# Attention scores as plain float32 products on 64-row halves of the TensorE array

## The chip, the cores and the metric

The kernel runs on one core of one Trainium2 chip. The metric is the device time of one execution in microseconds. A core has five engines that matter here: TensorE (PE; its weight loads are listed apart as PEld), VectorE (DVE), ScalarE (ACT), GpSimd (POOL) and SyncE (SP), whose queue issues most of the DMA transfers.

## The reference

Block-causal attention over 8 batches of 8 heads, 576 positions and 64 features, and behind it a feed-forward network on the 4608 tokens of 512 features, with 2048 hidden features and a leaky activation with a slope per hidden feature.

```python
scores = scale * np.matmul(q, k.transpose(0, 1, 3, 2))     # scale = 1/8
mask = block_i >= block_j                                  # blocks of 64 positions
scores = np.where(mask, scores, -1000000000.0)
scores = scores - np.max(scores, axis=-1, keepdims=True)
attn = np.exp(scores)
attn = attn / (np.sum(attn, axis=-1, keepdims=True) + 1e-09)
out = np.matmul(attn, v)
...
h = x @ w_in
g = np.maximum(h, 0.0) + alpha * np.minimum(h, 0.0)
return (g @ w_out).astype(np.float32)
```

Everything is float32. q and k are scaled so that the scores are large enough for their rounding to be seen in the output.

## The kernel before

**Tiling.** The 64 heads are taken as 32 pairs (p = 0 to 31, four pairs to a batch). A pair lies on the 128 partitions: features of head 0 on 0 to 63, of head 1 on 64 to 127. Queries are taken in tiles of 128 (j = 0 to 3), and a tile j sees the first w = 128 (j + 1) keys. The last 64 queries of both heads form one more tile, j = 4, which sees all 576 keys: q comes from the host with these 64 columns of head 0 zero on the rows of head 1 and the reverse, so that one product with all 128 rows gives both heads.

**One query tile** (`query_tile`): scores into PSUM banks, row maximum on VectorE (L897 or L903), exponential on ScalarE (L906), row sums and reciprocal on VectorE, scaling by it on GpSimd (L914), transposes on TensorE (L922), copies to PTF. Then `values` multiplies the transposed probabilities with v (L1022): both heads of a pair, each on its own 64 columns of the array, as plain float32 products, and the result goes to xT, from where the feed-forward network takes it.

**Scores of most pairs.** A float32 product can be made of several products of the faster type float32r, if each operand is split into a rounded part and a remainder. `prep` loads q and k of a pair, writes QH (q/8 rounded, ScalarE, L781), QL (the remainder, VectorE, L783), KH (ScalarE, L786) and KL (GpSimd, L787), and then moves these by ten DMA transfers on SP's queue (`move`, L791) into two stacked tiles Q and K. There each head has all 128 rows of the array: one product (L890, i = 0) adds QH KH and QL KH, a second (i = 1) adds QH KL and, from its other 64 rows, the mask (`late` and `here`, written once into Q and K by `fixed_parts`). So a score tile j below 4 takes two float32r products per head. The tile j = 4 takes six of 288 columns straight from QH, QL, KH and KL (L952).

**Scores of the first pairs.** So that the start need not wait for all this, the tiles j = 0 and 1 of pairs 0 to 3, and all tiles of pair 0, are made as plain float32 products (`plain`): q is loaded into parts of xT that are free then, each head in its own 256 columns with zeros on the other head's rows (`early_loads`, `rest`), k is scaled by 1/8 (`scaled`: on VectorE for pairs 0 and 1, L805, on GpSimd for the others, L807), the product uses all 128 rows of the array (L885), and the mask is added by a small bfloat16 product (L886). The last tile of pair 0 is at L946.

**Banks.** There are eight PSUM banks; at most 7 of them may be held by attention, 2 by hidden activations, 2 by output sums. For j < 2 the two heads' scores share a bank, for j = 2 and 3 each has its own.

**The order.** All work is entered as operations with an engine, an estimated cost, a priority, what they read and write, and the buffers that they claim. A planner (`Plan.schedule`) simulates the engines with these costs and issues on each engine the ready operation with the lowest priority number. A table, SHIFTS, adds an offset to the priority of single operations; its keys are the priorities before the offset. The costs of products on part of the array are estimated by `c_apart(n, more)`. The part of the feed-forward network with the hidden slices f = 0 to 5 of 16 (FA = 6, in chunks of 256 tokens, `ffn1` L623 and `ffn2` L660) is issued between the attention products while later pairs are still being worked on; the rest (L701, L660) runs after attention, from about 575 us.

Weights arrive as 64-bit numbers and are converted by `to_f32` (the DMA at L505, then VectorE and ScalarE), two blocks at a time.

Of the kernel before, what the change touches and what calls it, by code (L numbers as in the profile page):

```python
# [373 lines left out]
def attn_ffn(ctx, tc, qT, kT, vT, w_in, w_out, alpha, out):  # L374
# [20 lines left out]
    nc.vector.memset(mask_l[0:1, 0:64], 1.0)  # L395
    nc.vector.memset(mask_r[0:1, :], NEG)
# [21 lines left out]
    KX = pool0.tile([P, 384], F32, name="KX")  # L418
# [3 lines left out]
    sp = att.enter_context(tc.tile_pool(name="sp", bufs=1))  # L422
# [20 lines left out]
    def rooms(pool, *kinds):  # L443
        for kind, n, shape, dt in kinds:
# [4 lines left out]
    rooms(st, ("qraw", 1, [QP], F32), ("kraw", 1, [S], F32), ("vraw", 1, [5, 2, D], F32), ("p", PB, [512], F32), ("pl", 1, [S], F32),  # L449
# [3 lines left out]
    late = const.tile([P, 8], F32, name="late")  # L453
    here = const.tile([P, 8], F32, name="here")
    nc.gpsimd.memset(late, 0.0)
    nc.gpsimd.affine_select(out=late, in_=late, pattern=[[1, 8]], base=64, channel_multiplier=-1,
                            compare_op=ALU.is_ge, fill=NEG)
    nc.gpsimd.memset(here, 0.0)
    nc.gpsimd.affine_select(out=here, in_=here, pattern=[[1, 8]], base=64, channel_multiplier=-1,
                            compare_op=ALU.not_equal, fill=1.0)  # L460

    def spread(t):

        ap = t[64:128]
        return bass.AP(ap.tensor, ap.offset, [ap.ap[0], [0, 2], [1, 8], [0, 64]])
# [302 lines left out]
    def twice(ap):  # L768
        return bass.AP(ap.tensor, ap.offset, [ap.ap[0], [0, 2], [1, SM]])

    def prep(p, pr):


        raw, kraw, vraw = Buf("qraw"), Buf("kraw"), Buf("vraw0" if p % 2 else "vraw")
        QH, QL, KH, KL, Q, K = (Buf(k) for k in ("QH", "QL", "KH", "KL", "Q", "K"))
        op("SP", 320, lambda: nc.sync.dma_start(out=raw(), in_=qT[p]), w=[raw], prio=pr)
        op("SP", 288, lambda: nc.sync.dma_start(out=kraw(), in_=kT[p]), w=[kraw], prio=pr)
        op("SP", 320, lambda: nc.sync.dma_start(out=vraw(), in_=vT[p]), w=[(vraw, 0), (vraw, 1)], prio=pr + VL)
        v_parts = vraw, [(vraw, 0), (vraw, 1)]

        op("ACT", c_act(QP, True), lambda: nc.scalar.activation(out=QH(), in_=raw(), func=AF.Copy, scale=0.125),  # L781
           r=[raw], w=[QH], prio=pr)
        op("DVE", c_dve(QP), lambda: nc.vector.scalar_tensor_tensor(  # L783
            out=QL(), in0=raw(), scalar=0.125, in1=QH().bitcast(F32), op0=ALU.mult, op1=ALU.subtract),
            r=[raw, QH], w=[QL], prio=pr)
        op("ACT", c_act(S, True), lambda: nc.scalar.copy(out=KH(), in_=kraw()), r=[kraw], w=[KH], prio=pr)  # L786
        op("POOL", c_pool(S), lambda: nc.gpsimd.tensor_tensor(  # L787
            out=KL(), in0=kraw(), in1=KH().bitcast(F32), op=ALU.subtract), r=[kraw, KH], w=[KL], prio=pr)

        def move(to, of, key, src, kb=128):  # L790
            op("SP", kb, lambda: nc.sync.dma_start(out=to().bitcast(F32), in_=of().bitcast(F32)), r=[src], w=[key], prio=pr)  # L791
        for h in range(2):
            hs, qs = slice(64 * h, 64 * h + 64), slice(SM * h, SM * h + SM)
            move(lambda qs=qs: Q()[0:64, :, qs], lambda hs=hs: twice(QH()[hs, :SM]), (Q, h, 0), QH, 256)
            move(lambda qs=qs: Q()[64:128, 0, qs], lambda hs=hs: QL()[hs, :SM], (Q, h, 1), QL)
            for i in range(2):
                ro = slice(64 * i, 64 * i + 64)
                move(lambda h=h, ro=ro: K()[ro, 2 * h], lambda hs=hs: KH()[hs, :SM], (K, h, i), KH)
            move(lambda h=h: K()[0:64, 2 * h + 1], lambda hs=hs: KL()[hs, :SM], (K, h, 2), KL)
        qk_parts = (Q, K, (QH, QL, KH, KL))  # L800
        return qk_parts, v_parts

# [6 lines left out]

    def early_loads():  # L810


        def zeros(engine, ps):
            for h in range(2):
                rows = slice(64 - 64 * h, 128 - 64 * h)
                engine.memset(xT[rows, ps, S + 256 * h:S + 256 * h + 256], 0.0)
        pr = E0 - 8
        op("DVE", 700, lambda: zeros(nc.vector, slice(0, 1)), w=[("zeros", 0)], prio=pr)
        op("POOL", 1600, lambda: zeros(nc.gpsimd, slice(1, NP)), w=[("zeros", p) for p in range(1, NP)], prio=pr)

        def tails():
            for h in range(2):
                nc.gpsimd.memset(KX[64 - 64 * h:128 - 64 * h, 256 + 64 * h:320 + 64 * h], 0.0)
        op("POOL", 400, tails, w=[("zeros", "tail")], prio=pr + 1)
        for p0, p1 in ((0, 1), (1, NP)):
            for h in range(2):
                hs = slice(64 * h, 64 * h + 64)
                op("SP", 64 * (p1 - p0), lambda h=h, hs=hs, p0=p0, p1=p1: nc.sync.dma_start(
                    out=xT[hs, p0:p1, S + 256 * h:S + 256 * h + 256],
                    in_=qT[p0:p1, hs, :256].rearrange("p r n -> r p n")), w=[("q", p, h) for p in range(p0, p1)], prio=pr)  # L830
        for ps, to, queue in (((0,), lambda: o_k()[:, :256], "ACTQ"), ((1, 2), lambda: o_k2().rearrange("p (i n) -> p i n", i=2), "SP"),
                              ((3,), lambda: KX[:, :256], "SP")):
            issuer = {"SP": nc.sync, "ACTQ": nc.scalar}[queue]
            op(queue, 128 * len(ps), lambda ps=ps, to=to, issuer=issuer: issuer.dma_start(
                out=to(), in_=kT[ps[0]:ps[-1] + 1, :, :256].rearrange("p r n -> r p n") if len(ps) > 1 else kT[ps[0], :, :256]),
                w=[("k", p) for p in ps], claim=[o_k] if ps == (0,) else [o_k2] if len(ps) > 1 else [], prio=pr + ps[0])
        for p in range(NP):
            scaled(p, 256, lambda p=p: plain_k[p]()[:, :256], ("k", p), pr + p)

    def early(p, pr):  # L840
        vraw = Buf("vraw0" if p % 2 else "vraw")
        op("SP", 128, lambda: nc.sync.dma_start(out=vraw()[:, :2], in_=vT[p, :, :2]), w=[(vraw, 0), (vraw, 1)], prio=pr + VE)
        return None, (vraw, [(vraw, 0), (vraw, 1)])

    def rest(pr):

        vraw = Buf("vraw")
        for h in range(2):
            hs = slice(64 * h, 64 * h + 64)
            op("SP", 64, lambda h=h, hs=hs: nc.sync.dma_start(out=xT[hs, 0, S + 256 * h:S + 256 * h + 256], in_=qT[0, hs, 256:512]),  # L850
               w=[("q", 0, h)], prio=pr)
        op("SP", 128, lambda: nc.sync.dma_start(out=o_k()[:, 256:512], in_=kT[0, :, 256:512]), w=[("k", 0, 1)], claim=[o_k], prio=pr)
        scaled(0, 256, lambda: o_k()[:, 256:512], ("k", 0, 1), pr)
        op("SP", 32, lambda: nc.sync.dma_start(out=klast(), in_=kT[0, :, 512:S]), w=[("k", 0, 2)], prio=pr)
        scaled(0, 64, klast, ("k", 0, 2), pr)
        for h in range(2):
            hs = slice(64 * h, 64 * h + 64)
            op("SP", 16, lambda h=h, hs=hs: nc.sync.dma_start(out=KX[hs, 256 + 64 * h:320 + 64 * h], in_=qT[0, hs, SM + 64 * h:SM + 64 * h + 64]),
               w=[("tail", h)], prio=pr)
        op("SP", 320, lambda: nc.sync.dma_start(out=vraw(), in_=vT[0]), w=[(vraw, 0), (vraw, 1)], prio=pr + VL)  # L860
        return None, (vraw, [(vraw, 0), (vraw, 1)])

    def query_tile(p, qk_parts, j, pr):
# [307 lines left out]
```

## Time and profile before

| | us |
|---|---|
| time, median of 3 runs | 1109.04 |
| lowest and highest of the runs | 1108.87, 1112.01 |
| span of the profiled execution | 1112.3 |
| attention stage with network work between | 0 to about 575 |
| rest of the network | about 575 to 1112 |

The profiled execution's own time is given by its span alone, 1112.3 us; it is near the highest of the three timed runs.

A page of the profile has the busy time of each engine, a strip of 40 slices of the span, the chain of work that ended last, and the costliest groups of instructions, named by line, engine, operation and tiles. A group `bank<-K,Q 128*128 128x512 f32 x4` is four instructions on an array of 128 rows by 128 columns with 512 moving columns. A float32 product stands as two records, a float32r product as one; the trace writes f32 for both. Products are pipelined, and the ends of their records are modelled: the distance from one start to the next is what a product costs.

### The profile page before, as it was taken

How to read it: one execution, taken by the hardware profiler on the slowest of the kernel's cores; microseconds unless marked ns; L12 is line 12 of the kernel's file. 1: busy time of each engine (PE TensorE's matmuls, PEld its weight loads, DVE VectorE, ACT ScalarE, POOL GpSimd, SP SyncE). 2: the span in 40 equal slices, each digit the busy share in tenths (PEclk: the TensorE clock that was granted, in tenths of full speed). 3: DMA queues.
4: the chain of work that ended last, by engine and by line, in shares of the span. 5: the costliest groups of instructions: out<-in, count | busy, mean ns of one | idle time of the engine just before them, and what ended most of it. 6: DMA issues, size and time to landing. Idle time of an engine off the chain costs nothing.

```text
span 1112.3 us, 21554 instructions
## 1 busy us (share of the span) xinstructions
PE 1091.3 (98%) x7342; PEld 949.8 (85%) x7342; DVE 700.1 (63%) x1651; ACT 627.4 (56%) x1740; POOL 600.2 (54%) x771
## 2 busy tenths in 40 slices
PE   7989999999999999999999999999999999999998
PEld 5668888888888888888888888889898989898987
DVE  7787666565565655756548997564747555555554
ACT  7878877675676676757655655343433434343432
POOL 5657657655656555555569985343434435252522
PEclk9999999999999999999999999999999999999999
DMA  7897787766476774738343523130303030312021
GB/s 219 239 260 226 198 244 187 208 186 183 127 203 189 192 209 124 230 103 244 80 148 114 165 90 103 43 114 1 115 1 114 1 114 7 108 39 77 1 76 39
DMA packets 75309, 147.92 MB, mean 133 GB/s; under 512 B 9792, under 2 KB 11840, under 8 KB 75200
## 3 DMA queue, kind: packets, MB, share of 16 engines
q1 hardware_dynamic: 74768, 146.28, 44.9%
q8 instruction: 58, 0.95, 0.4%
q14 instruction: 51, 0.42, 0.1%
q10 hardware_dynamic: 432, 0.27, 0.1%
HBM read 68.40 MB, written 29.36 MB: 88 GB/s over the span
## 4 chain that ended last, share of the span: by engine, by line
PE 89%; DVE 3%; DMA 3%; POOL 2%; issue 1%; SPq 1%; ACT 0%; DVEq 0%; POOLq 0%
PE bank L660 34%; PE bank L701 20%; PE bank L623 12%; PE bank L1022 7%; PE bank L890 6%; PE bank L922 6%; DMA raw<-in_w_in 2%; PE bank L952 2%; PE bank L978 1%; DVE m L507 1%; DMA raw<-in_w_out 1%; POOL xl L611 0%; POOL w L529 0%; DVE m L519 0%; DVE bank L512 0%
## 5 line engine op out<-in xcount | busy, mean ns | idle before, releaser
L643 POOL TENSOR_TENSOR gl<-g,gh 128x256 fp32r<-128x256 f32 x288 | 220.9, 776 | 303.7 <-ACT gh L640 159.3
L701 PEld LDWEIGHTS bank<-X,w 128*128 128x128 f32 x1890 | 246.1, 189 | 16.6 <-DVE X L529 1.2
L701 PE MATMUL bank<-X,w 128*128 128x256 f32 x1890 | 250.7, 281 | 1.1 <-DVE X L529 1.0
L660 PE MATMUL bank<-w,gh 128*128 128x512 f32 x720 | 225.3, 394 | 0.0
L634 ACT ACTIVATE g<-bank 128x256 f32<-128x256 f32 x288 | 109.5, 384 | 197.2 <-DVE bank L714 164.0
L914 POOL TENSOR_SCALAR p<-p,ri 128x128 f32<-128x128 f32 (+3 forms) x256 | 137.6, 552 | 126.7 <-DVE ri L912 56.4
L636 DVE SCALAR_TENSOR_TENSOR g<-g,oal,bank 128x256 f32<-128x256 f32 x288 | 134.3, 476 | 57.9 <-ACT g L634 55.3
L640 ACT CAST gh<-g 128x256 fp32r<-128x256 f32 x288 | 116.4, 407 | 89.7 <-DVE g L636 85.5
L906 ACT ACTIVATE p<-bank,nm 128x256 f32<-128x256 f32 (+3 forms) x256 | 133.8, 530 | 34.9 <-DVE nm L903 15.5
L660 PE MATMUL bank<-w,gl 128*128 128x512 f32 x360 | 141.6, 393 | 0.0
L714 DVE TENSOR_TENSOR bank<-bank,g 128x256 f32<-128x256 f32 x180 | 75.0, 428 | 102.7 <-PE bank L701 99.0
L660 PE MATMUL bank<-wa,gh 128*128 128x512 f32 x432 | 139.6, 404 | 0.0
L660 PEld LDWEIGHTS bank<-w,gh 128*128 128x128 f32 x720 | 124.0, 188 | 17.4
L623 PE MATMUL bank<-xh,wa 128*128 128x256 f32 x864 | 128.1, 287 | 0.9 <-DVE PTF L996 0.7
L623 PEld LDWEIGHTS bank<-xh,wa 128*128 128x128 f32 x864 | 113.8, 190 | 4.5 <-DVE PTF L996 1.1
L922 PE MATMUL bank<-ident,p 128*128 128x128 f32 x640 | 100.6, 278 | 9.3 <-POOL p L914 7.4
L890 PE MATMUL bank<-K,Q 128*128 128x512 f32 (+1 forms) x472 | 100.1, 332 | 0.8 <-DMA K<-KL 0.7
L922 PEld LDWEIGHTS bank<-ident,p 128*128 128x128 f32 x640 | 76.0, 142 | 21.6 <-POOL p L914 12.1
L710 DVE TENSOR_TENSOR g<-bank,g 128x256 f32<-128x256 f32 x135 | 56.6, 421 | 59.6 <-PE bank L701 58.4
L1022 PE MATMUL bank<-PTF,vraw 128*64 128x320 f32 (+3 forms) x768 | 94.1, 384 | 0.0
L903 DVE TENSOR_REDUCE nm<-bank 128x1 f32<-128x512 f32 (+1 forms) x128 | 76.4, 617 | 23.0 <-PE bank L890 19.0
L660 PE MATMUL bank<-wa,gl 128*128 128x512 f32 x216 | 85.5, 396 | 0.5 <-POOL gl L643 0.4
(111 smaller groups left out, 1677.8 us busy)
## 6 DMA issues: line engine op xcount, KB each, us to landing
Q<-QH SPq DMA_DIRECT2D x62, 256.0 KB, 3.8
K<-KH SPq DMA_DIRECT2D x124, 128.0 KB, 3.7
vraw<-in_v SPq DMA_DIRECT2D x32, 320.0 KB, 4.2
qraw<-in_q SPq DMA_DIRECT2D x31, 320.0 KB, 3.8
xd<-xT SPq DMA_DIRECT2D x8, 1152.0 KB, 6.7
part<-o SPq DMA_DIRECT2D x36, 256.0 KB, 3.0
xb<-xd SPq DMA_DIRECT2D x9, 1024.0 KB, 5.4
m<-part SPq DMA_DIRECT2D x36, 256.0 KB, 2.9
```

What stands on the lines that cost most here:

```text
L623: nc.tensor.matmul(hp()[:, :n], ww()[:, 0, cc * P:(cc + 1) * P], x()[:, cc, :n], start=(i == 0 and cc == 0), stop=(i == 2 and cc == NCC - 1))
L634: op("ACT", c_act(CHA), lambda: nc.scalar.activation(out=g(), in_=hp()[:, ts], func=AF.Relu, scale=-1.0), r=[hp], w=[g], prio=FP)
L636: op("DVE", c_dve(CHA) + 60, lambda: nc.vector.scalar_tensor_tensor(out=g(), in0=g(), scalar=oal[:, f:f + 1], in1=hp()[:, ts], op0=ALU.mul ...
L640: op("ACT", c_act(CHA, True), lambda: nc.scalar.copy(out=gh(), in_=g()), r=[g], w=[gh], prio=FP)
L643: op("POOL", c_pool(CHA), lambda: nc.gpsimd.tensor_tensor(out=gl(), in0=g(), in1=gh().bitcast(F32), op=ALU.subtract), r=[g, gh], w=[gl], p ...
L660: nc.tensor.matmul(acc(), a()[:, ts], ww(), start=(first and i == 0), stop=(last and i == 2))
L701: nc.tensor.matmul(bank()[:, :CHA], W()[:, i, 256 * at + P * c:256 * at + P * c + P], B()[:, j, CHA * c:CHA * c + CHA], start=(n == 0), st ...
L890: nc.tensor.matmul(o, Q()[:, i, qs], K()[:, 2 * h + i, :w], start=(i == 0), stop=(i == 1))
L906: op("ACT", 238 + w / 1.2, lambda h=h, t=t: nc.scalar.activation(out=t()[:, :w], in_=sb[h]()[:, off[h]:off[h] + w], func=AF.Exp, bias=nm() ...
L914: op("POOL", 244 + w / 1.2, lambda h=h: nc.gpsimd.tensor_scalar(out=pts[h]()[:, :w], in0=pts[h]()[:, :w], scalar1=ri()[:, h:h + 1], scalar ...
L922: nc.tensor.transpose(out=tp()[:, base + c * P:base + (c + 1) * P], in_=pts[h]()[:, c * P:(c + 1) * P], identity=ident)
L1022: nc.tensor.matmul(ob()[rows[h], a - q0:q1 - q0], V()[:, c, h, :], moving, start=(c == 0), stop=(c == cs[-1][0]))
```

## The change

All scores become plain float32 products, and each head uses only its own 64 rows of the array: head 0 rows 0 to 63, head 1 rows 64 to 127, with no zero padding. The loaded q and k are used where they lie. The splitting into QH, QL, KH, KL, the ten moves, the stacked tiles Q and K with their fixed parts, the zero fills, and the separate path of pair 0 (`rest`) are gone; k is scaled by 1/8 in place for every pair. The mask is added for every tile j < 4 by two bfloat16 products on the same halves of rows, for which mask_l and mask_r now have a filled row in each half. Both heads' products of a tile are one operation of the planner, with an estimated cost of `c_apart(w, CHANGE)`, CHANGE = 300, and each head has its own bank for every j. The tile j = 4 becomes two plain products on the whole array, of 512 and of 64 columns. q and k have two buffers each. Priorities, SHIFTS and all other costs stay.

```diff
     nc.vector.memset(mask_r, 0.0)
-    nc.vector.memset(mask_l[0:1, 0:64], 1.0)
-    nc.vector.memset(mask_r[0:1, :], NEG)
+    for r in (0, 64):
+        nc.vector.memset(mask_l[r:r + 1, 0:64], 1.0)
+        nc.vector.memset(mask_r[r:r + 1, :], NEG)
...
-    rooms(st, ("qraw", 1, [QP], F32), ("kraw", 1, [S], F32), ("vraw", 1, [5, 2, D], F32), ("p", PB, [512], F32), ("pl", 1, [S], F32),
+    rooms(st, ("qraw", 2, [QP], F32), ("kraw", 2, [S], F32), ("vraw", 1, [5, 2, D], F32), ("p", PB, [512], F32), ("pl", 1, [S], F32),
...
-    rooms(sp, ("QH", 1, [QP], F32R), ("QL", 1, [QP], F32R), ("KH", 1, [S], F32R), ("KL", 1, [S], F32R),
-          ("Q", 2, [2, 2 * SM], F32R), ("K", 2, [4, SM], F32R))
...
+    def region(p, a, b):
+        return xT[:, p, S + a:S + b]
+
     def early_loads():
         pr = E0 - 8
...
+        op("SP", 128, lambda: nc.sync.dma_start(out=region(0, 0, 256), in_=qT[0, :, :256]), w=[("R", 0, 0)], prio=pr)
+        op("ACTQ", 128, lambda: nc.scalar.dma_start(out=region(0, 256, 512), in_=kT[0, :, :256]), w=[("R", 0, 1)], prio=pr)
+        for i, src, at in ((1, kT, 256), (0, qT, 0)):
+            op("SP", 384, lambda src=src, at=at: nc.sync.dma_start(out=xT[:, 1:NP, S + at:S + at + 256], in_=src[1:NP, :, :256].rearrange("p r n -> r p n")),
+               w=[("R", p, i) for p in range(1, NP)], prio=pr + 1)
         for p in range(NP):
-            scaled(p, 256, lambda p=p: plain_k[p]()[:, :256], ("k", p), pr + p)
+            scaled(p, 256, lambda p=p: region(p, 256, 512), ("R", p, 1), pr + p)
...
+    def prep(p, pr):
+        vraw = Buf("vraw0" if p % 2 else "vraw")
+        raw, kraw = Buf("qraw"), Buf("kraw")
+        op("SP", 288, lambda: nc.sync.dma_start(out=kraw(), in_=kT[p]), w=[kraw], prio=pr)
+        op("SP", 320, lambda: nc.sync.dma_start(out=raw(), in_=qT[p]), w=[raw], prio=pr)
+        scaled(p, S, kraw, kraw, pr)
+        op("SP", 320, lambda: nc.sync.dma_start(out=vraw(), in_=vT[p]), w=[(vraw, 0), (vraw, 1)], prio=pr + VL)
+        return ((lambda a, b: raw()[:, a:b]), (lambda b: kraw()[:, :b]), (lambda: raw()[:, SM:]), (lambda: kraw()[:, SM:]), [raw, kraw]), (vraw, [(vraw, 0), (vraw, 1)])
...
+            sb = [Buf("bank", "att"), Buf("bank", "att")]
+
+            def qk_plain():
+                rows = slice(0, 64), slice(64, 128)
+                for h in range(2):
+                    nc.tensor.matmul(sb[h]()[:, :w], q_main(j * P, (j + 1) * P)[rows[h]], k_main(w)[rows[h]], start=True, stop=False)
+                for h in range(2):
+                    nc.tensor.matmul(sb[h]()[:, w - 64:w], mask_l[rows[h]], mask_r[rows[h]], start=False, stop=True)
...
+            op("PE", c_apart(w, CHANGE), qk_plain, r=parts, w=[(sb[0], 0), (sb[1], 1), "scores"], claim=[*pts, nm, s, sp, ri], prio=pr)
             for h in range(2):
                 t = pts[h]
-                if not shared:
-                    op("DVE", c_dve(w), lambda h=h: nc.vector.tensor_reduce(
-                        out=nm()[:, h:h + 1], in_=sb[h]()[:, off[h]:off[h] + w], axis=AX.X, op=ALU.max, negate=True),
-                        r=[(sb[h], h)], w=[(nm, h)], prio=pr)
+                op("DVE", c_dve(w), lambda h=h: nc.vector.tensor_reduce(
+                    out=nm()[:, h:h + 1], in_=sb[h]()[:, :w], axis=AX.X, op=ALU.max, negate=True),
+                    r=[(sb[h], h)], w=[(nm, h)], prio=pr)
...
+        K8 = (0, 512), (512, S)
         sb = [Buf("bank", "att"), Buf("bank", "att")]
 
         def qk8():
-            if plain:
-                for hf, rhs in ((0, plain_k[0]()), (1, klast())):
-                    nc.tensor.matmul(sb[hf]()[:, :K8[hf][1] - K8[hf][0]], KX[:, 256:384], rhs, start=True, stop=True)
-                return
-            QH, QL, KH, KL = stacked
-            for hf in range(2):
-                ks = slice(hf * HW, (hf + 1) * HW)
-                for i, (q, k) in enumerate(((QH, KH), (QL, KH), (QH, KL))):
-                    nc.tensor.matmul(sb[hf]()[:, :HW], q()[:, SM:], k()[:, ks], start=(i == 0), stop=(i == 2))
+            for hf, rhs in ((0, k_main(SM)), (1, k_last())):
+                nc.tensor.matmul(sb[hf]()[:, :K8[hf][1] - K8[hf][0]], q_last(), rhs, start=True, stop=True)
...
-        qk_parts, v_parts = prep(p, pr - 4.5) if p else rest(pr - 4.5)
+        qk_parts, v_parts = prep(p, pr - 4.5)
```

More of the change, by code (lines that the diff above doesn't have):

```diff
@@ L417, in attn_ffn @@
     PTF = [pool0.tile([P, 2, PW], F32, name=f"PTF{i}") for i in range(2)]
-    KX = pool0.tile([P, 384], F32, name="KX")
     PT4 = [pool0.tile([P, 2, 64], F32, name=f"PT4{i}") for i in range(2)]
@@ L764, in store @@
         op("SP", 256, lambda: nc.sync.dma_start(out=to[t:t + P, :], in_=o()), r=[o], w=[(key, t)], prio=FP)
[L768 to L801, printed above, removed]
     def scaled(p, n, k, key, prio):
@@ L821, in tails @@
[L821 to L836, printed above, removed]
+        op("SP", 128, lambda: nc.sync.dma_start(out=region(0, 0, 256), in_=qT[0, :, :256]), w=[("R", 0, 0)], prio=pr)
@@ L842, in early @@
         op("SP", 128, lambda: nc.sync.dma_start(out=vraw()[:, :2], in_=vT[p, :, :2]), w=[(vraw, 0), (vraw, 1)], prio=pr + VE)
[L843 to L861, printed above, removed]
@@ L863, in query_tile @@
-    def query_tile(p, qk_parts, j, pr):
-        plain = p < NP and j < 2 or p == 0
-        Q, K, stacked = qk_parts or (None, None, None)
-        def keys(h):
-            if plain:
-                return [("zeros", p), ("q", p, h), ("k", p), *[("k", p, 1)] * (j > 1), *[("k", p, 2), ("tail", h), ("zeros", "tail")] * (j > 3), *held_by[p]]
-            if j > 3:
-                return list(stacked)
-            return [(Q, h, i) for i in range(2)] + [(K, h, i) for i in range(3)] + [("fixed", k, i) for k in "QK" for i in range(2)]
+        return (lambda a, b: region(p, a, b), lambda b: region(p, 256, 256 + b), None, None, [("R", p, 0), ("R", p, 1)]), (vraw, [(vraw, 0), (vraw, 1)])
@@ L875, in query_tile @@
+    def query_tile(p, qk_parts, j, pr):
+        q_main, k_main, q_last, k_last, parts = qk_parts
+        if p < NP and j < 2:
+            parts = [*parts, *[("x", 1, p, x, n) for x in range(2) for n in range(2)]]
         nm, sp, ri = Buf("nm"), Buf("sp"), Buf("ri")
@@ L877, in query_tile @@
         if j < 4:
-            shared = j < 2
-            sb = [Buf("bank", "att")] * 2 if shared else [Buf("bank", "att"), Buf("bank", "att")]
-            off = [0, w if shared else 0]
-            def qk(h):
-                o = sb[h]()[:, off[h]:off[h] + w]
-                if plain:
-                    nc.tensor.matmul(o, xT[:, p, S + 256 * h + j % 2 * P:S + 256 * h + j % 2 * P + P], plain_k[p]()[:, :w], start=True, stop=False)
-                    nc.tensor.matmul(o[:, w - 64:w], mask_l, mask_r, start=False, stop=True)
-                    return
-                qs = slice(SM * h + j * P, SM * h + (j + 1) * P)
-                for i in range(2):
-                    nc.tensor.matmul(o, Q()[:, i, qs], K()[:, 2 * h + i, :w], start=(i == 0), stop=(i == 1))
+            sb = [Buf("bank", "att"), Buf("bank", "att")]
@@ L891, in query_tile @@
+            def qk_plain():
[4 more added lines that the diff above has]
+                    nc.tensor.matmul(sb[h]()[:, w - 64:w], mask_l[rows[h]], mask_r[rows[h]], start=False, stop=True)
             s = Buf("s")
             pts = [Buf("p") for _ in range(2)]
-            for h in range(2):
-                op("PE", (c_mm(4 * w) + c_mm(64)) if plain else 2 * c_mm(w), lambda h=h: qk(h), r=keys(h), w=[(sb[h], h), "scores"], claim=[pts[h], nm, s, sp, ri],
-                   prio=pr)
```

46 lines of the change are left out of this document (3 added, 43 removed).

## The prediction

> **What bounds the kernel.** I read the page first: the span, the busy time of TensorE (PE) and how it lies over the span.
>
> ```profile
> span 1112.3 us, 21554 instructions
> PE 1091.3 (98%) x7342; PEld 949.8 (85%) x7342; DVE 700.1 (63%) x1651; ACT 627.4 (56%) x1740; POOL 600.2 (54%) x771
> ```
>
> TensorE misses 21 us of 1112.3. The view by windows says where, and the waits of TensorE say for what (total, times, longest).
>
> ```profile
> 0.00:50.00 50.00, 40.79 (x245) 29.23 (x247) 40.51 (x109) 37.10 (x104) 31.64 (x55) 1.00 0.80 232
> 50.00:100.00 50.00, 43.42 (x297) 34.38 (x294) 40.81 (x102) 40.10 (x111) 30.94 (x37) 0.97 0.87 243
> 100.00:575.00 475.00, 475.00 (x3488) 409.77 (x3487) 284.43 (x754) 321.90 (x972) 276.11 (x391) 1.00 0.63 178
> ```
>
> ```profile
> PE bank L922 <- POOL p L914: 7.4, 4, 2.9
> ```
>
> In each row: PE, PEld, DVE, ACT, POOL busy, then granted clock, DMA share, GB/s. From 100 us to the end of attention (575 us) TensorE has no idle time; VectorE has 191 us to spare, ScalarE 153, GpSimd 199, the DMA engines a third. All real idle time, 100 - 40.79 - 43.42 = 15.8 us, lies before 100 us, where the DMA engines are 80% busy and more. So **every product added after 100 us is paid in full**, and work taken from other engines or from the DMA queue is worth something only before it.
>
> **What the scores cost now.** The timeline gives it by differences of starts (a busy time reaches into the next instruction; only starts count). Columns: start, busy time, then the group.
>
> ```profile
> 301.77 0.64 PE L623 MATMUL bank<-xh,wa 128*128 128x256 f32 x4
> 302.25 0.64 PE L623 MATMUL bank<-xl,wa 128*128 128x256 f32 x4
> 302.82 2.16 PE L1022 MATMUL bank<-PTF,vraw 128*64 128x320 f32 x16
> ...
> 305.68 0.74 PE L660 MATMUL bank<-wa,gh 128*128 128x512 f32 x2
> 306.26 0.40 PE L660 MATMUL bank<-wa,gl 128*128 128x512 f32 x1
> 306.49 0.56 PE L890 MATMUL bank<-K,Q 128*128 128x128 f32 x4
> 306.89 0.35 PE L952 MATMUL bank<-KH,QH 128*128 128x288 f32 x1
> ...
> 307.73 1.78 PE L890 MATMUL bank<-K,Q 128*128 128x512 f32 x8
> 309.35 0.63 PE L660 MATMUL bank<-wa,gh 128*128 128x512 f32 x2
> 309.81 0.40 PE L660 MATMUL bank<-wa,gl 128*128 128x512 f32 x1
> ...
> 327.57 0.86 PE L890 MATMUL bank<-K,Q 128*128 128x384 f32 x4
> ...
> 328.27 1.11 PE L623 MATMUL bank<-xh,wa 128*128 128x256 f32 x8
> ```
>
> Two split products of 512 columns take 309.81 - 309.35 = 0.46 us, so a score tile (two heads, two products each) takes 0.93 at j=3; j=2 takes 328.27 - 327.57 = 0.70; j=1 like four 256-wide products, 302.25 - 301.77 = 0.48; j=0 306.89 - 306.49 = 0.40; the last tile (six products of 288) 307.73 - 306.89 = 0.84. **A pair costs 3.35 us.**
>
> **What they will cost.** The kernel already has plain float32 products, in the first pair; the last row below is of the mask's sort (L886).
>
> ```profile
> 17.86 0.60 PE L885 MATMUL bank<-KX,xT 128*128 128x256 f32 x2
> 18.30 0.19 PE L886 MATMUL bank<-mask_r,mask_l 128*128 128x64 bf16 x1
> ...
> 26.07 1.02 PE L885 MATMUL bank<-o,xT 128*128 128x512 f32 x2
> 26.93 0.19 PE L886 MATMUL bank<-mask_r,mask_l 128*128 128x64 bf16 x1
> 26.96 1.10 PE L885 MATMUL bank<-o,xT 128*128 128x512 f32 x2
> ...
> 28.18 0.81 PE L885 MATMUL bank<-o,xT 128*128 128x384 f32 x2
> 28.83 0.19 PE L886 MATMUL bank<-mask_r,mask_l 128*128 128x64 bf16 x1
> ```
>
> One such product takes 0.86 us for 512 columns, 0.65 for 384, 0.44 for 256, so 0.22 for 128: nearly four times a split one, as two records. Before, a tile has four split products; after, one plain product per head, which is the same array time only if the two heads run side by side. No row shows two row halves at once. The nearest is L1022, whose two heads use two column halves:
>
> ```profile
> 302.82 0.49 PE L1022 MATMUL bank<-PTF,vraw 128*64 128x320 f32 x2
> 303.14 0.71 PE L1022 MATMUL bank<-PTF,vraw 128*64 128x320 f32 x4
> 303.41 0.71 PE L1022 MATMUL bank<-PTF,vraw 128*64 128x320 f32 x4
> 305.36 0.39 PE L1022 MATMUL bank<-PTF,vraw 128*64 128x128 f32 x4
> ```
>
> Two records begin together, 0.27 us apart from the next two: 320 columns at the rate of one head alone (0.44/256 x 320 / 2 = 0.275). So side by side it is, and I take it over to rows; the other end, one after the other, is a rival below.
>
> The same rows price **the change between whole array and halves**. Entry: 302.82 - 302.25 = 0.57 where four 256-wide products take 0.48, +0.09. First pair: 0.32 instead of 0.27, +0.05, its loads uncovered. Exit: 305.68 - 305.36 = 0.32 for two pairs of 128 columns worth 0.22, +0.10. First product behind: 306.26 - 305.68 = 0.58 where 0.46 is usual, +0.12. Together 0.36. A row half loads 128 columns, not 64:
>
> ```profile
> L660 PEld LDWEIGHTS bank<-wa,gh 128*128 128x128 f32 x432 | 75.0, 189 | 11.9 <-issue 0.3 <-DVE sp L910 0.2 <-ACT xT L1026 0.2
> L1022 PEld LDWEIGHTS bank<-PTF,vraw 128*64 128x64 f32 x768 | 49.6, 137 | 36.1 <-issue 2.7 <-ACT pl L965 0.7 <-ACT p L906 0.5
> ```
>
> That is 0.05 more (189 against 137 ns): 0.41. I take 0.38. The ends: nothing, since another half-wide product pays nothing, and 0.5 with a second load uncovered:
>
> ```profile
> 316.09 0.27 PE L987 MATMUL bank<-ident,pl 128*64 128x128 f32 x1
> 316.12 0.48 PE L890 MATMUL bank<-K,Q 128*128 128x256 f32 x2
> ```
>
> (0.03 us from the transpose at L987 to the next product.)
>
> The row first: 0.10 us is lost between the last half-width product and the next whole one. [...]
>
> Sum for a pair from the fifth on (28): products 0.86 + 0.65 + 0.44 + 0.22 = 2.17; masks, 26.96 - 26.93 = 0.03 a tile (two side by side), 0.12; changes 4 x 0.38 = 1.52; last tile, now 512 + 64 columns plain on the whole array, 0.86 + 0.11, with its load 1.0. That is 4.81, **+1.46 us a pair, 40.9 us**. Pairs 1 to 3 have only j=2, 3 and the last tile here: 3.33 against 2.47, +2.6 in all. Pair 0 was plain already, both heads one after the other on a zero-padded array: 2.33 against 3.14, -0.8. Its early tiles and those of pairs 1 to 3: 1.44 before, 1.48 after, nothing. Together +42.7 us, with 120 new changes. Where two score tiles adjoin, no change lies between; of seven tiles from 300 to 330 us two do (the eight products at 307.73 are j=3 and j=2): 120/7 x 0.38 = **-6.5**.
>
> **What else moves.** Gone are ten SP moves per pair, the casts and the remainder KL; added is one scaling of k on GpSimd, half of KL's cost, and a second reduction for j < 2 on VectorE.
>
> ```profile
> L787 POOL TENSOR_TENSOR KL<-kraw,KH 128x576 fp32r<-128x576 f32 x31 | 47.8, 1540 | 25.3 <-ACT KH L786 25.3
> L972 POOL TENSOR_SCALAR pl<-pl,ri 128x576 f32<-128x576 f32 x32 | 25.9, 809 | 13.9 <-DVE ri L971 7.7 <-ACT gh L640 2.2 <-PE bank L922 1.5
> ```
>
> ```profile
> Q<-QH SPq DMA_DIRECT2D x62, 256.0 KB, 3.8
> K<-KH SPq DMA_DIRECT2D x124, 128.0 KB, 3.7
> ```
>
> After 100 us all this is covered by TensorE's own queue and worth nothing; if that cover went, VectorE's spare 191 us would still hold the extra reductions. Before 100 us it counts: the moves share the queue and engines with the weights, for which the chain of waits pays longest, and right behind which TensorE waits:
>
> ```profile
> 72.26 10.62 DMA raw<-in_w_in
> 84.73 1.33 PE L922 MATMUL bank<-ident,p 128*128 128x128 f32 x8 [2.92 <-POOL p L914]
> ```
>
> The 2.92 us go, and so may others; the end is 15.8, the other end nothing. I take half, **-8**. At the start all of k and q for pairs 1 to 3 come in two larger loads; the bytes are the same. Scaling k now stands ahead of the scores where the moves stood: on GpSimd the remainders gl (L643) queue behind it, and for those the FFN products wait, but it is shorter than the KL that it replaces; on TensorE, which works in order, all products queue behind a score tile whose k is late, as they do today behind one whose moves are late.
>
> The order is computed from costs and the offsets in SHIFTS, which stay while the work under them changes; a j < 2 tile now takes two of seven banks. The row from 100 to 575 us says no waits today; the other end is as much as before 100 us, 15.8. Nearest is zero; I take **+3**.
>
> 42.7 - 6.5 - 8 + 3 = **+31 us**. The profiled span, 1112.3, stands 3.3 above the median of the runs, 1109.0 (they reach 1112.0); the difference is put on the median: **1140 us**.
>
> **Rivals.**
> 1. *Row halves change for free*, like L987: 42.7 - 120 x 0.38 = -2.9, and -8 + 3: -8 us, 1101, **faster**. It decides below 0.08 us a change (8/103). For it: only the row at L987; against: every L1022 group pays. 0.12.
> 2. *The heads overlap by one record only.* Each head has two records; if starts keep the program's order, head 1 begins with head 0's second record, three record times instead of two: 0.43 + 0.32 + 0.22 + 0.11 = 1.08 us a pair, 32 pairs, +35: 1175. Against: at 302.82 the first two records begin together, and nothing is left over at the end. 0.06. [...]
> 3. *No overlap*, the change not doing what it says: 2.17 x 32 = +69 more: 1209. 0.05.
> 4. *The order loses its cover* and TensorE waits in the attention stage as it did before 100 us: +13 on the forecast, 1153; for it, banks and offsets; against, VectorE and GpSimd get less to do in a stage where they already have 191 and 199 us to spare. 0.10.
>
> **Numbers.** The forecast has 0.67: with 0.5 a change it gives 1152, with 0.2 and all early idle time gone 1114. Range 1108 to 1170: it holds the forecast, the fourth rival and the border of the others. About 0.3%, 3.3 us, can be told from no change. Faster: rival 1 and a little of the forecast's tail, 0.13; within 0.3% 0.05; slower 0.82.
>
> **What would show it.** Right: score tiles on 64 rows whose records begin in twos, 0.43 us apart at 512 columns; about 0.1 us lost on either side of each; no idle TensorE from 100 us on; its idle time before 100 us near 8 us; attention ending some 30 us later, and the rest unchanged. Wrong: whole-array products starting on time behind a score tile (rival 1), single starts (2, 3), waits of TensorE on GpSimd or VectorE after 100 us (4). A clock below 1.00 after 100 us would be a cause that I have not counted.

## The result and the profile after

| | us | against the kernel before |
|---|---|---|
| before, median of 4 runs (the 1109.04 above is that of three of them) | 1109.72 | |
| predicted | 1140.0 (1108 to 1170) | +31 |
| changed, median of 4 runs (1142.04 to 1142.61) | 1142.59 | +32.9, ratio 1.029, interval 1.0274 to 1.0305 |

The change makes the kernel slower by 2.9%. First the page of the changed kernel, then its stages by windows (PE, PEld, DVE, ACT, POOL busy; granted clock, DMA share, GB/s) and its waits.

```profile
span 1140.8 us, 21209 instructions
PE 1121.0 (98%) x7516; PEld 915.6 (80%) x7516; DVE 680.0 (60%) x1682; ACT 594.9 (52%) x1676; POOL 563.2 (49%) x762
```

```profile
0.00:50.00 50.00, 40.76 (x261) 26.34 (x262) 39.09 (x119) 34.27 (x104) 26.78 (x47) 1.00 0.53 176
50.00:100.00 50.00, 47.14 (x335) 33.55 (x334) 39.29 (x101) 38.92 (x106) 33.21 (x44) 1.00 0.45 151
100.00:575.00 475.00, 475.00 (x3429) 356.98 (x3428) 257.55 (x760) 283.64 (x886) 230.79 (x369) 1.00 0.27 88
```

```profile
PE bank L789 <- DVE xT L741: 2.9, 1, 2.9
PE bank L816 <- POOL p L808: 2.7, 2, 2.6
PE bank L672 <- DVE m L490: 1.6, 1, 1.6
```

TensorE is again without a gap from 100 to 575 us, while every other engine has less to do than before and the DMA share there falls from 0.63 to 0.27. So from 100 us on, what was taken away was hidden, and what was added is on TensorE.

The profile of before that the prediction used had waited more than most of its executions. So the same kernel was profiled once more; this is the second profile of before in what follows.

> The kernel before once more, for a second profile. The profile shown has a span 2 to 3 us over the median of the runs, with 21.0 us of idle TensorE and a stretch at half clock. Theory (that execution waited longer than most): a span of 1107 to 1109 with 15 to 18 us of idle TensorE, so that the changed kernel, with 19.8, idles about 3 us more, not less. Rival: the same 21 us.

Measured: 1110.48 us, ratio 0.9987 (0.9971 to 1.0003), a span that belongs to the median, and 18.0 us of idle TensorE, as the theory had it:

```profile
span 1108.3 us, 21554 instructions
PE 1090.3 (98%) x7342; PEld 949.6 (86%) x7342; DVE 699.8 (63%) x1651; ACT 627.4 (57%) x1740; POOL 600.3 (54%) x771
```

```profile
0.00:50.00 50.00, 40.74 (x249) 29.30 (x251) 41.17 (x110) 37.60 (x104) 32.61 (x56) 0.97 0.82 235
50.00:100.00 50.00, 46.44 (x330) 37.92 (x327) 44.30 (x110) 42.41 (x119) 34.42 (x42) 0.97 0.91 259
```

Against it the span grew by 32.5 us: 30.7 are busy TensorE (1121.0 - 1090.3) and 1.8 idle TensorE (19.8 against 18.0). Before 100 us TensorE idles 12.1 us in the changed kernel, 12.8 here, 15.8 in the first profile. Part of the busy time of before is work at half clock: the traces hold two granted clocks, 1.00 and 0.50, and a mean of 0.97 over 50 us is 3 us at 0.50 (0.03 x 50 / 0.5). In the first profile, where such a stretch lies from 86.0 to 89.4 us, a product of 288 columns takes 0.24 us in it (88.41 - 87.44 for four) and 0.13 at full clock (307.60 - 307.07). Both windows above have such a stretch, worth 1.5 us of work each by an estimate from that; the changed kernel's record has none there. So the work on TensorE grew by 31 to 34 us.

Attention ends when the prediction said: the last product of `values` starts at 596.0 us, against 566.9 in the second profile of before, 29 us later. What follows takes 3 us more.

Now a score tile from close by, in the timeline of the changed kernel (L789 a plain product on a row half, L791 its mask, L838 the last tile).

```profile
314.48 0.39 PE L631 MATMUL bank<-wa,gl 128*128 128x512 f32 x1
314.80 0.49 PE L789 MATMUL bank<-kraw,qraw 64*128 64x128 f32 x4
315.12 0.20 PE L791 MATMUL bank<-mask_r,mask_l 64*128 64x64 bf16 x2
315.25 1.29 PE L838 MATMUL bank<-kraw,qraw 128*128 128x512 f32 x4
316.47 1.13 PE L789 MATMUL bank<-kraw,qraw 64*128 64x512 f32 x4
317.43 0.20 PE L791 MATMUL bank<-mask_r,mask_l 64*128 64x64 bf16 x2
317.46 0.90 PE L789 MATMUL bank<-kraw,qraw 64*128 64x384 f32 x4
318.19 0.20 PE L791 MATMUL bank<-mask_r,mask_l 64*128 64x64 bf16 x2
318.31 0.73 PE L631 MATMUL bank<-wa,gh 128*128 128x512 f32 x2
318.89 0.40 PE L631 MATMUL bank<-wa,gl 128*128 128x512 f32 x1
```

A narrower window shows which of the four records of the tile at 316.47 begin together:

```profile
316.47 0.70 PE L789 MATMUL bank<-kraw,qraw 64*128 64x512 f32 x2
```

Two of the four records begin together, and the whole tile of both heads takes 317.43 - 316.47 = 0.96 us: one head's 0.86 and 0.10 of uncovered loads (their records start with the products, at 316.47). So two heads take the array time of one. The borders are where time is lost. Entry: 314.80 - 314.48 = 0.32 for a product that otherwise takes 0.23, +0.09. First loads: +0.10, as said. Exit: 318.31 - 318.19 = 0.12 for a mask that otherwise takes 0.03 (317.46 - 317.43), +0.09. First product behind: 318.89 - 318.31 = 0.58 for 0.46, +0.12. **Together 0.40 us for a stretch.** Where two score tiles adjoin (317.46), the second still takes 318.19 - 317.46 = 0.73 for 0.65, as its weight loads start only with the mask product, at 317.43: adjoining saves 0.31, not all.

### The profile page after: what moved, and what is told of

It reads as the page before. It is cut to its first block, busy times and chain, and to the rows that moved or that the text cites. A ratio compares the mean times of both kernels' runs of the same rounds, so it can differ in the third digit from the quotient of the medians.

```text
span 1140.8 us, 21209 instructions
## 1 busy us (share of the span) xinstructions
PE 1121.0 (98%) x7516; PEld 915.6 (80%) x7516; DVE 680.0 (60%) x1682; ACT 594.9 (52%) x1676; POOL 563.2 (49%) x762
## 4 chain that ended last, share of the span: by engine, by line
PE 92%; DVE 3%; ACT 2%; DMA 1%; POOL 1%; issue 1%; ACTq 0%; DVEq 0%; POOLq 0%
PE bank L631 33%; PE bank L672 19%; PE bank L594 12%; PE bank L909 8%; PE bank L789 8%; PE bank L816 7%; PE bank L838 3%; PE bank L865 1%; DVE xh L580 1%; DVE g L607 0%; DMA xT<-in_k 0%; DVE X L500 0%; DMA raw<-in_w_in 0%; DVE bank L483 0%; PE bank L874 0%
## 5 line engine op out<-in xcount | busy, mean ns | idle before, releaser
L614 POOL TENSOR_TENSOR gl<-g,gh 128x256 fp32r<-128x256 f32 x288 | 218.5, 768 | 341.5 <-ACT gh L611 169.7
L808 POOL TENSOR_SCALAR p<-p,ri 128x384 f32<-128x384 f32 (+3 forms) x256 | 134.5, 542 | 153.3 <-DVE ri L806 68.3
L800 ACT ACTIVATE p<-bank,nm 128x512 f32<-128x512 f32 (+3 forms) x256 | 133.5, 529 | 44.7 <-DVE nm L797 39.4
L797 DVE TENSOR_REDUCE nm<-bank 128x1 f32<-128x512 f32 (+3 forms) x256 | 113.5, 483 | 64.5 <-PE bank L791 63.9
L631 PE MATMUL bank<-wa,gh 128*128 128x512 f32 x432 | 142.8, 412 | 0.0
L816 PE MATMUL bank<-ident,p 128*128 128x128 f32 x640 | 95.7, 279 | 4.0 <-POOL p L808 2.7
L789 PE MATMUL bank<-kraw,qraw 64*128 64x512 f32 (+1 forms) x480 | 95.4, 487 | 0.0
L816 PEld LDWEIGHTS bank<-ident,p 128*128 128x128 f32 x640 | 73.1, 142 | 23.0 <-POOL p L808 9.2
L631 PEld LDWEIGHTS bank<-wa,gh 128*128 128x128 f32 x432 | 73.7, 189 | 16.8 <-issue 5.5
```

The source lines that it names most:

```text
L614: op("POOL", c_pool(CHA), lambda: nc.gpsimd.tensor_tensor(out=gl(), in0=g(), in1=gh().bitcast(F32), op=ALU.subtract), r=[g, gh], w=[gl], p ...
L631: nc.tensor.matmul(acc(), a()[:, ts], ww(), start=(first and i == 0), stop=(last and i == 2))
L789: nc.tensor.matmul(sb[h]()[:, :w], q_main(j * P, (j + 1) * P)[rows[h]], k_main(w)[rows[h]], start=True, stop=False)
L797: op("DVE", c_dve(w), lambda h=h: nc.vector.tensor_reduce(out=nm()[:, h:h + 1], in_=sb[h]()[:, :w], axis=AX.X, op=ALU.max, negate=True), r ...
L800: op("ACT", 238 + w / 1.2, lambda h=h, t=t: nc.scalar.activation(out=t()[:, :w], in_=sb[h]()[:, :w], func=AF.Exp, bias=nm()[:, h:h + 1], a ...
L808: op("POOL", 244 + w / 1.2, lambda h=h: nc.gpsimd.tensor_scalar(out=pts[h]()[:, :w], in0=pts[h]()[:, :w], scalar1=ri()[:, h:h + 1], scalar ...
```

## The experiments

Times are medians; a ratio is to the kernel before as it ran beside the variant (1110.0 to 1111.2 us), with its interval. The changed kernel was timed in one group of runs, so differences to its 1142.6, or between two variants, are known to some 2 to 4 us. First, three runs on the array itself.

**A second change of mode in each tile.** Head 0's mask goes over the whole array, between the products and head 1's mask on the halves.

```diff
-                for h in range(2):
-                    nc.tensor.matmul(sb[h]()[:, w - 64:w], mask_l[rows[h]], mask_r[rows[h]], start=False, stop=True)
+                nc.tensor.matmul(sb[0]()[:, w - 64:w], mask_l, mask_r, start=False, stop=True)
+                nc.tensor.matmul(sb[1]()[:, w - 64:w], mask_l[rows[1]], mask_r[rows[1]], start=False, stop=True)
```

> The changed kernel, with head 0's mask product on the whole array, between the products on the two row halves and head 1's mask on its half: one more change of array mode and back in each of the 128 score tiles. [...] Rival (changes cost next to nothing and the array time is what grew): only one mask product of 0.03 us more a tile, +4 us, 1147.

Measured: 1173.32 us, ratio 1.0568 (1.0543 to 1.0593): +30.7 on the changed kernel, or 0.24 a tile. The timeline has the parts (L790 is the mask on the whole array):

```profile
300.72 0.92 PE L789 MATMUL bank<-kraw,qraw 64*128 64x384 f32 x4
301.57 0.20 PE L790 MATMUL bank<-mask_r,mask_l 128*128 128x64 bf16 x1
301.71 0.20 PE L791 MATMUL bank<-mask_r,mask_l 64*128 64x64 bf16 x1
301.71 0.71 PE L789 MATMUL bank<-kraw,qraw 64*128 64x256 f32 x4
```

From the first product to the mask 0.85, where 0.65 and 0.10 of loads would do: +0.10 for leaving the halves. From that mask to the next on the halves 0.14: +0.11 for coming back, and the mask's own 0.03. So a change of mode costs time of its own, 0.24 us there and back around a short mask; the rival's 1147 is out.

**No halves at all.** Both heads use all 128 rows, one after the other; the scores mix the heads.

```diff
-                    nc.tensor.matmul(sb[h]()[:, :w], q_main(j * P, (j + 1) * P)[rows[h]], k_main(w)[rows[h]], start=True, stop=False)
+                    nc.tensor.matmul(sb[h]()[:, :w], q_main(j * P, (j + 1) * P), k_main(w), start=True, stop=False)
...
-                    nc.tensor.matmul(sb[h]()[:, w - 64:w], mask_l[rows[h]], mask_r[rows[h]], start=False, stop=True)
+                    nc.tensor.matmul(sb[h]()[:, w - 64:w], mask_l, mask_r, start=False, stop=True)
...
-            op("PE", c_apart(w, CHANGE), qk_plain, r=parts, w=[(sb[0], 0), (sb[1], 1), "scores"], claim=[*pts, nm, s, sp, ri], prio=pr)
+            op("PE", 2 * (c_mm(4 * w) + c_mm(64)), qk_plain, r=parts, w=[(sb[0], 0), (sb[1], 1), "scores"], claim=[*pts, nm, s, sp, ri], prio=pr)
```

> The changed kernel, but each head's plain product and mask on all 128 rows of the array, one head after the other; the operands' other 64 rows are not zeroed, so the scores mix the two heads. No changes of mode for the scores, and no two heads side by side. Theory (heads run side by side on row halves, a change costs 0.38 us): array time +2.17 us a pair, masks +0.12, 32 pairs: +73; 104 changes gone: -40; together +33, 1176 (1168 to 1184). Rival (heads do not run side by side, or by one record only): -36, 1107, or -1, 1142. Rival (changes cost nothing): +73, 1216.

Measured: 1178.88 us, ratio 1.0615 (1.0599 to 1.0631): +36.3 on the changed kernel, +33 expected. Its timeline:

```profile
309.62 1.88 PE L789 MATMUL bank<-kraw,qraw 128*128 128x512 f32 x4
311.34 0.22 PE L791 MATMUL bank<-mask_r,mask_l 128*128 128x64 bf16 x2
311.40 0.74 PE L816 MATMUL bank<-ident,p 128*128 128x128 f32 x5
```

Two heads take 311.34 - 309.62 = 1.72 us, twice 0.86, and the product behind the masks starts 0.06 later, without a loss. By the sum above, side by side saves some 73 us of array time and masks, and the changes give 40 of them back, which leaves 33. The run measures only the difference of the two. Its busy TensorE is 1162.6 us, 41.6 more than in the changed kernel, and its idle TensorE 14.1, 5.7 less; so the work grew by more than 33, and the total of 36 comes as near as it does because the idle time fell.

**Fewer changes.** Scores of two tiles of a pair in one piece.

```diff
+            other = j - 1 if front is not None and j in (3, 1) else None
...
+            if other is not None:
+                two = front[other] = (Buf("nm"), Buf("sp"), Buf("ri"), Buf("s"), [Buf("p") for _ in range(2)], [Buf("bank", "att") for _ in range(2)])
+                sb2 = two[5]
+                op("PE", c_apart(w, CHANGE) + c_apart(w - P), lambda: (qk_plain(), qk_plain(other, w - P, sb2)), r=parts,
+                   w=[(sb[0], 0), (sb[1], 1), (sb2[0], 0), (sb2[1], 1), "scores"],
+                   claim=[*pts, nm, s, sp, ri, *two[:4], *two[4]], prio=pr)
```

> The changed kernel, with the scores of tiles j = 3 and 2 of a pair issued as one piece, and those of j = 1 and 0 likewise (not the early tiles of pairs 0 to 3 on their own, which go the same way where they are issued). The trace of the changed kernel has 104 stretches of score products on row halves; about 55 to 60 should be left. Theory: 45 to 49 changes less at 0.38 us, -17 us, 1125 (1122 to 1130), minus what four banks taken at once cost. Rival (changes cost nothing): 1143, or more because of the banks.

Measured: 1141.75 us, ratio 1.0278 (1.0263 to 1.0293): 0.8 us faster, not 17. A miss. The page and the two longest waits of TensorE:

```profile
span 1140.4 us, 21178 instructions
PE 1115.5 (98%) x7516; PEld 917.1 (80%) x7516; DVE 679.5 (60%) x1682; ACT 590.5 (52%) x1676; POOL 562.9 (49%) x762
```

```profile
PE bank L827 <- POOL p L819: 4.8, 4, 2.6
PE bank L795 <- DVE xT L741: 2.5, 1, 2.5
```

The stretches on row halves went from 104 to 66, counted over the timeline (the early tiles stay single). At 0.31 that is 12 us; busy TensorE fell by 5.5 only, and idle TensorE rose from 19.8 to 24.9, 4.7 of it before 100 us, so that the waits took back nearly all of the 5.5. Four banks of seven taken at once fit that, but were not tested apart. The clock of 0.97 between 50 and 100 us accounts for some 1.5 us of the busy time; about 5 us of the expected fall are not located.

**The last tile alone**, on the kernel before.

```diff
-            QH, QL, KH, KL = stacked
-            for hf in range(2):
-                ks = slice(hf * HW, (hf + 1) * HW)
-                for i, (q, k) in enumerate(((QH, KH), (QL, KH), (QH, KL))):
-                    nc.tensor.matmul(sb[hf]()[:, :HW], q()[:, SM:], k()[:, ks], start=(i == 0), stop=(i == 2))
+            q, k = raws
+            for hf, (k0, k1) in enumerate(K8):
+                nc.tensor.matmul(sb[hf]()[:, :k1 - k0], q()[:, SM:], k()[:, k0:k1], start=True, stop=True)
```

> The kernel before, with the last tile (j = 4) of pairs 1 to 31 alone made as in the changed kernel: two plain products of 512 and 64 columns from the loaded q and k (the factor 1/8 is left out there). Theory: 1.0 us in place of 0.84 on TensorE, 31 pairs, +5 us on 1109.7, 1115 (1112 to 1117). Rival (the last tile is hidden, or its reductions of 512 and 64 columns make VectorE late): no change, or over 1120.

Measured: 1122.13 us, ratio 1.011 (1.0092 to 1.0127): +12, over the theory's 5 and in the rival's second range, over 1120. But not for the rival's reason: TensorE does not wait more.

```profile
span 1119.5 us, 21453 instructions
PE 1101.0 (98%) x7280; PEld 944.0 (84%) x7280; DVE 699.8 (63%) x1651; ACT 627.4 (56%) x1740; POOL 603.7 (54%) x771
```

Idle TensorE is 18.5 us, as in the second profile of before (18.0), and busy TensorE is 10 to 11 us more than in either. The distances from start to start over the whole trace (idle time left out, time at half clock counted half) sum to 26 us for the last tiles before and 32 here, so the tile itself costs 6 more; the other 4 or more are spread over the products around it. Why these became dearer is open. The miss raised the question of the next runs: does any change of the work also cost what the offsets in SHIFTS had gained for the old order?

**The moves.** First put back into the changed kernel, with nobody waiting for them:

```diff
         scaled(p, S, kraw, kraw, pr)
+        if p:
+            Q, K = Buf("Q"), Buf("K")
+            def move(to, of, key, src, kb=128):
+                op("SP", kb, lambda: nc.sync.dma_start(out=to(), in_=of()), r=[src], w=[key], prio=pr)
...
```

> The changed kernel with the ten moves of each pair from 1 to 31 put back on SP's queue, from the loaded q and k into tiles that nobody reads: 1.5 MB a pair, no wait of TensorE on them. Theory (without the moves the weights come earlier, which is worth something before 100 us): +3 to +8 us on 1142.6, all of it as idle TensorE before 100 us. Rival (the idle time before 100 us is set by other waits): no change, within 2 us.

Measured: 1150.91 us, ratio 1.0368 (1.035 to 1.0385): +8.3. Where, the windows say:

```profile
0.00:50.00 50.00, 40.35 (x264) 25.05 (x264) 37.72 (x116) 34.00 (x103) 26.60 (x47) 1.00 0.81 241
50.00:100.00 50.00, 44.50 (x277) 32.35 (x277) 37.51 (x93) 32.73 (x89) 29.21 (x38) 0.90 0.84 234
```

Idle TensorE before 100 us is 15.2 us, 3.1 more; and a clock of 0.90 over 50 us is 10 us at half speed, up to 5 us of work lost. Busy time with that taken out is the same in both, so the moves cost time by waits and by the clock that goes with them. (The moves also hold the buffers of q and k longer; that was not tested apart.) Then the moves taken out of the kernel before (mask left out, heads mixed):

```diff
-        for h in range(2):
-            hs, qs = slice(64 * h, 64 * h + 64), slice(SM * h, SM * h + SM)
-            move(lambda qs=qs: Q()[0:64, :, qs], lambda hs=hs: twice(QH()[hs, :SM]), (Q, h, 0), QH, 256)
...
-                    nc.tensor.matmul(o, Q()[:, i, qs], K()[:, 2 * h + i, :w], start=(i == 0), stop=(i == 1))
+                    nc.tensor.matmul(o, Q[i]()[:, qs], K[i]()[:, :w], start=(i == 0), stop=(i == 1))
```

> The kernel before without the ten moves: the two products per head read QH, QL, KH and KL (two buffers each) where they lie, with all 128 rows; the mask, which came with the moved tiles, is left out, and the scores mix the two heads. Same products on TensorE, same splitting, 1.5 MB a pair less on the DMA engines. Theory: -4 to -8 us, 1102 to 1106, from idle TensorE before 100 us. Rival: no change, 1108 to 1112.

Measured: 1111.17 us, ratio 1.0005 (0.9994 to 1.0016): nothing, as the rival said. Here too TensorE idles less before 100 us, 11.7 us against 15.8 and 12.8, but more after it, 7.9 against 5.2. Two runs that seem to contradict each other.

**The offsets.** Both kernels with the table emptied (`SHIFTS = {}`).

> The kernel before with an empty table SHIFTS. The offsets were set for this order of work: some 3 to 15 us slower than 1109.7. Read together with the changed kernel without offsets. Theory (array time of the score tiles makes the difference): the gap between the two without offsets is as it is with them, 25 to 36 us. Rival (the offsets fit the kernel before and cost the changed one time): the gap shrinks below 20 us.

> The changed kernel with an empty table SHIFTS. Theory: within 6 us of 1142.6, and 25 to 36 us above the kernel before without offsets. Rival (the offsets misfit and cost time): 10 us or more faster than 1142.6.

Measured: before 1125.44, ratio 1.0135 (1.0118 to 1.0152); changed 1150.20, ratio 1.0368 (1.0351 to 1.0384). The offsets are worth 15.7 us to the kernel before and 7.6 to the changed one. The gap without them is 24.8 us, just under the theory's band, and not below the rival's 20: most of the difference is work, and 8 of the 33 us, give or take 3, go with the offsets. The pages, before and then changed, say in what form:

```profile
span 1125.4 us, 21543 instructions
PE 1100.5 (98%) x7342; PEld 953.6 (85%) x7342; DVE 703.8 (63%) x1651; ACT 629.3 (56%) x1740; POOL 600.5 (53%) x771
```

```profile
span 1148.4 us, 21167 instructions
PE 1130.0 (98%) x7516; PEld 915.2 (80%) x7516; DVE 684.6 (60%) x1682; ACT 595.9 (52%) x1676; POOL 564.2 (49%) x762
```

Without offsets the change adds 29.5 us of busy TensorE and takes away 6.5 of idle; with them it adds 30.7 and 1.8 (against the first profile of before it adds 29.7 and takes away 1.2). So the work is nearly the same either way, and most of the 8 us is idle time: the offsets take 4 to 7 us of it from the kernel before (24.9 to 21.0 and 18.0) and none from the changed one (18.4 to 19.8). What they are worth to the changed kernel is busy time, 9.0 us: without them its score tiles make 118 stretches on row halves, not 104, and some 3 us more are lost at half clock. Then the two open questions, without offsets:

> The kernel before with an empty table SHIFTS and without the ten moves (as in the run without moves: the mask is left out and the scores mix the two heads). To be read against the kernel before with an empty table, 1125.4. Theory (the moves cost time before 100 us, and in the run without moves this was given back because the offsets no longer fitted the order): 5 to 10 us faster, 1115 to 1120. Rival (the moves are hidden in the kernel before, whatever the order): within 3 us of 1125.

> The kernel before with an empty table SHIFTS and the last tile of pairs 1 to 31 as two plain products (the factor 1/8 is left out there). To be read against the kernel before with an empty table, 1125.4. Theory (of the 12 us that this tile cost with the offsets, 5 are its work and 7 the misfit of the offsets): +5, 1128 to 1133. Rival (the tile itself costs 12 us, by its work or its reductions): 1135 to 1140.

Measured: without moves 1115.04, ratio 1.0029 (1.0016 to 1.0042), 10.4 faster than 1125.44; last tile 1130.61, ratio 1.0172 (1.0138 to 1.0205), 5.2 slower than it, give or take 4. Both numbers are the theory's. For the last tile its reason is not shown: the tile itself costs 5 us more by the distances of starts (6 with the offsets), and all work on TensorE some 8 more, against which less time at half clock (0.93 instead of 0.83 between 50 and 100 us) and 1.8 us less idle time stand. So that 5 of the 12 us are work and 7 a misfit of the offsets is not what the traces say: in both pairs of profiles the work grew by 8 us or more.

For the moves, the windows of the kernel before without offsets:

```profile
0.00:50.00 50.00, 44.09 (x266) 31.38 (x267) 39.33 (x112) 38.22 (x109) 31.94 (x56) 1.00 0.87 231
50.00:100.00 50.00, 40.62 (x213) 30.16 (x211) 38.19 (x87) 34.15 (x86) 28.46 (x33) 0.83 0.90 240
```

and without the moves as well:

```profile
0.00:50.00 50.00, 43.77 (x265) 30.35 (x266) 40.16 (x113) 37.17 (x112) 32.21 (x55) 1.00 0.59 179
50.00:100.00 50.00, 44.52 (x303) 35.68 (x302) 42.73 (x102) 39.49 (x108) 37.83 (x43) 0.97 0.45 144
```

Idle TensorE before 100 us falls from 15.3 to 11.7 us, and the time at half clock from 17 us (0.17 x 50 / 0.5) to 3, worth up to 7: together 10.6 of the 12.0 us by which these two profiled executions differ. So the moves do cost time early where nothing was fitted around them, and nearly nothing in the kernel with its offsets. Whether the offsets had hidden that cost, or lose some of their worth as soon as the work is another, these runs do not tell apart; the later idle time of the run without moves but with offsets speaks for a share of the second.

**An earlier start** of the changed kernel: the early loads of pairs 1 to 3 ahead of the first weights.

```diff
-               w=[("R", p, i) for p in range(1, NP)], prio=pr + 1)
+               w=[("R", p, i) for p in range(1, NP)], prio=pr)
```

> The changed kernel with the early loads of k and q of pairs 1 to 3 at the priority of pair 0's, ahead of the first block of weights (in the changed kernel an offset of +1.5 in SHIFTS for the priority -11 puts them behind it, and the first scores wait until 6.28 us for k, against 4.34 in the kernel before). Theory: the first scores about 2 us earlier, -2 us, 1140.6. Rival: the weights come as much later and TensorE waits for them instead, no change or up to +2.

Measured: 1146.28 us, ratio 1.0319 (1.0306 to 1.0333): 3.7 slower, more than the rival said. The first scores did start earlier:

```profile
5.37 1.23 PE L789 MATMUL bank<-xT 64*128 64x256 f32 x4 [1.98 <-DVE xT L741]
```

0.9 us earlier than 6.28, and idle before 100 us fell by 2.0 us; the time came back elsewhere, as busy TensorE (1126.0 against 1121.0; a stretch of 3.4 us at half clock, at 638 us, is 1.7 of it, the rest is not located). One priority of two loads moves the total by as much as a term of the prediction.

None of the variants is faster than the kernel before. By these numbers plain products on halves don't with two changes a pair either: 2.17 + 0.12 + 0.76 + 1.0 = 4.05 us against 3.35; all four tiles in one stretch would make it 3.67 by the same sum, take eight banks where attention has seven, and wasn't tried.

## Why the prediction was right, and where two errors met

- **What bounds the kernel:** TensorE alone, after 100 us. Right: no idle time there in either kernel, and DVE, ACT, POOL and DMA relief in that stage came to nothing. "All real idle time" before 100 us is too much said: 15.8 of the 21.0 us lie there, the other 5.2 behind 575 us.
- **Heads side by side on row halves:** right. Records begin in twos, 0.96 us a tile of 512 columns; the same heads one after the other on the whole array take 1.72 a tile and cost the kernel +36 (+33 was computed). Rivals 2 and 3 fall.
- **0.38 us a change:** right, as an estimate carried over from column halves; for row halves 0.40 is read from the rows after, 0.09 of it at the entry and 0.09 at the exit, and +30.7 for 128 more changes around a short mask. Rival 1 falls. What the array does in these 0.09 us, no run shows.
- **Adjoining tiles, -6.5:** too small. Counted over the timeline, 24 of 128 tiles adjoin another (17 expected), at 0.31 each, -7.4; and at 15 borders a score stretch meets one of `values` directly, which the sum didn't have: by the rows one loss of 0.09 and one uncovered load of 0.10 fewer, 0.2 each, -3, an estimate. That makes the work 42.7 - 7.4 - 3 = 32.3, against 36.2 predicted; the profiles say 31 to 34, the busy time alone 30.7.
- **Moves gone, -8:** the size holds by itself (8.3 and 10.4 in the two runs that isolate it), but not for this kernel: before 100 us TensorE idles only 0.7 us less than in the second profile of before, and loses some 3 us less at half clock.
- **Order, +3:** the step that failed. "Nearest is zero" took the absence of waits from 100 to 575 us for the price of the order. There are none there after the change either; the idle time that replaces the early one lies behind 575 us (7.7 us after 100 us, against 5.2). Without offsets the change saves 6.5 us of idle TensorE, near the -5 that the two last terms give together; with them it adds 1.8, or takes away 1.2 against the first profile. So what the sum most likely lacks is that the offsets had already taken idle time out of the kernel before, which the change could then no longer save. No term priced that; the 15.8 us of the other end were put at +3.

So the total was met, +32.9 for +31, because two errors met: busy TensorE grew by 30.7 where 36.2 was predicted (2 to 5 us of that is work, the rest the half clock of before), and idle TensorE came out at +1.8 for -5. That is luck in the number; the mechanism of the main term, two heads at the price of one and a price at every border, is shown. Rival 4 named the order as a cause, and placed its waits in the wrong stage.

## What to carry to other kernels

Work that leaves idle engines earns nothing while one engine has no gaps: price a change by the starts on that engine, stretch by stretch. Using part of the array side by side saves array time, but each stretch of it costs a fixed amount at its borders (here 0.4 us, as much as some 240 float32 columns), so it pays for long stretches and not for short ones strewn between other products. And where an order was fitted to the work, part of what any edit seems to cost is the fit: compare both versions without it before blaming the edit (here taking out the moves was worth 0 with the fitted order and 10 us without), and compare busy and idle time apart, since a total can agree for another reason.

## What the runs showed of the hardware

Idle TensorE early went with a lower clock: in the kernel before without offsets, 9.4 us of it between 50 and 100 us came with a mean clock of 0.83, up to another 8.5 us of work. The recorded clock is either 1.00 or 0.50; in the first profile of before it is 0.50 from 86.0 to 89.4 us, with TensorE busy throughout, behind an idle gap of 2.92 us that ended at 84.73. Leaving aside the end of the program, the fourteen traces have 16 stretches at 0.50, of 3.4 us or two or three times that, and in the 3.4 us ahead of each TensorE idles 1.6 to 2.7 us (2.1 in this profile). Not every such gap has one behind it: the same profile idles 2.40 us before 22.23 us, and its clock stays at 1.00 from there to 86.0 us. What sets the clock, no run isolates.

The clock's record begins at 14.3 us in the first profile of before and at 16.4 in that of the changed kernel. Until then products take about twice as long: a score tile of 256 columns 7.29 - 6.28 = 1.01 us, against 320.67 - 320.13 = 0.54 later.

Two heads' records begin together, at 316.47, although the program gives head 0's product first; in what order the engine gets them, no run shows.
